# Transnormer attention and a squared-ReLU MLP: the normalised rows turned by VectorE in 32×32 blocks, the product with k^T·v in column strips, and the first loads split by halves of the partitions

## The chip, the cores and the metric

The kernel runs on one core of a Trainium2 chip. The metric is the device time in microseconds of one execution; less is better. TensorE (PE) multiplies matrices and writes to PSUM, VectorE (DVE) and ScalarE (ACT) work on SBUF and PSUM, GpSimd (POOL) does a few set-up steps here, and transfers are issued from the queues of SyncE (SP), ScalarE and GpSimd.

## The reference

All inputs are float32 but the two weight matrices of the second part and its scalars, which arrive as float64.

```python
# q, k, v: (8 batches, 8 heads, 576 positions, 64); g_norm: (64,)
kv  = einsum('bhsd,bhse->bhde', k, v)
out = einsum('bhsd,bhde->bhse', q, kv)
rms = sqrt(mean(out * out, axis=-1) + 1e-6)
x   = (out / rms * g_norm).transpose(0, 2, 1, 3).reshape(4608, 512)
h   = x @ w_in                    # (512, 2048)
g   = s * max(h, 0)**2 + b
res = g @ w_out                   # (2048, 512) -> (4608, 512)
```

## The kernel before

The 4608 rows of x are cut into 36 chunks of 128 rows, and four chunks make a unit; there are nine units. A unit's x is kept transposed in one tile, `xT` (channels on the partitions, four blocks of 128 channels; 512 rows along the free axis)[...]. `mm1` multiplies it with w_in, `mm2` multiplies the squared ReLU with w_out. From the second unit on, both are done with a seven-product scheme on 2×2 blocks, whose sums VectorE forms (`x_sums`, `sums_w_in`); unit 0's first product is done plainly (`mm1_plain`), in 16 slots of 16 PE instructions, because it has to start before the weights are all there.

For a chunk c, `attention(c)` gives three steps.

- `turn` transposes the chunk's q on TensorE (four 128×128 transposes) and copies the result to `qT`.
- `product` multiplies `qT` with `bd_kv`, a block-diagonal tile which holds k^T·v of two heads in each of its four 128×128 blocks. A chunk within one batch takes four matmuls; a chunk that lies in two batches (every ninth) takes eight, with 64 columns of `qT` each (L345). Then it normalises: the square on ScalarE (L354), the sum over a head on VectorE (L356), the root on ScalarE (L359), the reciprocal and the multiplication on VectorE (L361, L362), into `xn`.
- `turn_x` transposes `xn` on TensorE (four transposes, L370) and copies the result into `xT` on ScalarE, with the factor `g_col` (L373).

`kv_product(b)` forms k^T·v of a batch from 72 small matmuls on 64×64 quarters of the array (L297), and copies it to `bd_kv`.

Every engine works through its instructions in the order in which the program writes them (the schedule is manual). During the units, the steps of the next unit's four chunks stand between the slots of `mm2` (the table `side` in `side_of`). At the start there is nothing to lie beside, so the order is written out by hand:

```python
kv_product(0); turn[0](); product[0](); turn[1](); product[1]()
turn[2](); turn_x[0](); turn[3](); product[2](); plus(0)
turn_x[1](); product[3](); slots0[0](); turn_x[2]()
run([(lo, 1), (shift, 1), (plus, 1)]); slots0[1](); turn_x[3]()
```

The weights arrive as float64 words in "raw tiles" of 1 MB, three of which fit at a time. Four steps make a float32 tile of one: `hi` (L160) and `lo` (L165) on ScalarE, `shift` (L169) and `plus` (L179) on VectorE; `plus` frees the buffer and sends the next load. Tiles 0 to 7 are w_in, 8 to 15 are w_out. `tile_at` says after which slot of unit 0 a tile is converted, `more_at` after which its sums are formed. `slots0[0]` needs tile 0 and chunks 0 and 1; `slots0[1]` needs tile 1; `slots0[2]` needs chunks 2 and 3.

The first transfers: `load_kv(0, i)` loads half of batch 0's k and v as four transfers of 288 KB, each to 64 partitions (r = 0 the lower half, r = 1 the upper); k is issued on SP's queue and v on ScalarE's. `load_q(c)` loads two chunks in four transfers, again to 64 partitions each. On GpSimd's queue `g_col` (two transfers), `s_col` and `b_col` are loaded; VectorE multiplies `b_sq` with `b_col` (L278) before it does anything for the attention.

Of the kernel before, what the change touches and what calls it, by code (L numbers as in the profile page):

```python
# [15 lines left out]
def kernel(  # L16
# [34 lines left out]
    nc = tc.nc  # L51
# [235 lines left out]

    def kv_product(b):

        ps = [ps_t.tile([P, 2, D], FP32, name="kv_ps", tag="t") for _ in range(2)]  # L290
        for i in range(2):
            kv = kv_in.pop((b, i))
            for j in range(R):
                for l in range(2):
                    for r in range(2):
                        rows = slice(r * HB, r * HB + HB)
                        nc.tensor.matmul(  # L297
                            ps[r][l * HB : l * HB + HB, i, :],
                            lhsT=kv[rows, 0, l, j, :],
                            rhs=kv[rows, 1, l, j, :],  # L300
                            start=(j == 0),
                            stop=(j == R - 1),
                        )
        for r in range(2):
            for l in range(2):
                ls = slice(l * HB, l * HB + HB)
                if b == 0 and l == 1:
                    nc.vector.tensor_copy(out=bd_kv[0][ls, 2 * r : 2 * r + 2, ls], in_=ps[r][ls])
                else:
                    nc.scalar.copy(bd_kv[b % 2][ls, 2 * r : 2 * r + 2, ls], ps[r][ls])  # L310

    xT = {}

    def attention(c, first=False, between=lambda: None):

        (b, _), (b1, _) = halves(c)
        st = {}

        def turn():
            if first:
                ps = ps_a.tile([P, NP, P], FP32, name="qT_ps", tag="x")
            else:
                ps = ps_t.tile([P, NP, P], FP32, name="qT_ps", tag="t")
            for p in range(NP):
                nc.tensor.transpose(ps[:, p, :], q_in[c][:, 2 * p : 2 * p + 2, :], ident)  # L327
            st["qT"] = attp.tile([P, NP, P], FP32, name="qT", tag="qT")
            if first:
                nc.vector.tensor_copy(out=st["qT"], in_=ps)  # L330
            else:
                nc.scalar.copy(st["qT"], ps)

        def product():
            if first:
                ps = bank_of("att", "xy"[c % 2]).rearrange("p b (m n) -> p (b m) n", m=2)
            else:
                ps = ps_a.tile([P, NP, P], FP32, name="x_ps", tag="x")
            for p in range(NP):
                if b == b1:  # L340
                    matmul(ps[:, p, :], st["qT"][:, p, :], bd_kv[b % 2][:, p, :], True, True)
                    continue
                for s in range(2):
                    half = slice(s * HB, s * HB + HB)
                    nc.tensor.matmul(  # L345
                        ps[half, p, :],
                        lhsT=st["qT"][:, p, half],
                        rhs=bd_kv[(b + s) % 2][:, p, :],
                        start=True,
                        stop=True,  # L350
                    )
            x = ps.rearrange("p c (l d) -> p (c l) d", l=2)
            st["xn"] = attp.tile([P, H, D], FP32, name="xn", tag="xn")
            nc.scalar.activation(st["xn"], x, AF.Square)  # L354
            ss = attp.tile([P, H], FP32, name="ss", tag="ss")
            nc.vector.reduce_sum(ss, st["xn"], axis=mybir.AxisListType.X)  # L356
            between()
            rms = attp.tile([P, H], FP32, name="rms", tag="rms")
            nc.scalar.activation(rms, ss, AF.Sqrt, bias=eps_col, scale=1.0 / D)  # L359
            inv = attp.tile([P, H], FP32, name="inv", tag="inv")  # L360
            nc.vector.reciprocal(inv, rms)  # L361
            nc.vector.tensor_tensor(  # L362
                out=st["xn"], in0=x, in1=inv.unsqueeze(2).to_broadcast((P, H, D)), op=ALU.mult
            )

        def turn_x():
            u, j = divmod(c, 4)
            ps = ps_t.tile([P, NP, P], FP32, name="xT_ps", tag="t")
            for p in range(NP):
                nc.tensor.transpose(ps[:, p, :], st["xn"][:, 2 * p : 2 * p + 2, :], ident)  # L370
# [4 lines left out]
        return [turn, product, turn_x]  # L375

    xs = {}

# [321 lines left out]
    def hi(n):  # L700
        fold_hi(blocks[n])
# [29 lines left out]
    between = [[], [], [(hi, 0), (lo, 0), (shift, 0)], [(hi, 1)]]  # L731

    def run(steps):
        for fn, n in steps:
            fn(n)

    turn, product, turn_x = zip(
        *(attention(c, True, lambda c=c: run(between[c])) for c in range(4))
    )
    kv_product(0)  # L740
    turn[0]()
    kv0p.release()
    gp = ctx.enter_context(tc.tile_pool(name="gp", bufs=NS))
    product[0]()
    turn[1]()
    product[1]()
    turn[2]()
    turn_x[0]()
    turn[3]()
    product[2]()  # L750
    plus(0)
    turn_x[1]()
    product[3]()
    slots0 = [slot for s in range(NS) for slot in mm1_plain(s)]
    slots0[0]()
    turn_x[2]()
    run([(lo, 1), (shift, 1), (plus, 1)])
    slots0[1]()
    turn_x[3]()
    run([(hi, 2), (lo, 2), (shift, 2), (plus, 2)])  # L760

    def side_of(u):

        if u + 1 >= U:
            return {}
        turn, product, turn_x = zip(*(attention(c) for c in range(4 * u + 4, 4 * u + 8)))
        side = {
            2: [turn[0]],
            3: [product[0]],
# [129 lines left out]
```

## Time and profile before

| | |
|---|---|
| median of 20 runs | 1012.0 us (1009.21 to 1015.22) |
| the profiled execution | 1011.98 us, of which 1010.2 us are the span of the core's work |
| PE busy | 978.3 us, 97% of the span |
| VectorE, ScalarE busy | 452.4 us (45%), 203.8 us (20%) |
| granted PE clock, mean | 0.995 |

The page gives busy times of one profiled execution, the chain of work that ended last, and groups of equal instructions. A timeline lists instructions in order, merged where one kind follows another; its columns are the start, the time to the end of the last one, the engine, the line, the tiles and the count. A float32 matmul stands in the records as two instructions, a transpose as one. The records of PE overlap, since matmuls are pipelined; what PE spends on a group is read from its start to the start of the next group.

### The profile page before, as it was taken

The page shows a single profiled execution, that of the slowest core. Times are in us where ns is not written, and L with a number is a line of the kernel's source. Part 1 is how long each engine was busy: PE and PEld are TensorE (multiplying, and loading weights), DVE is VectorE, ACT ScalarE, POOL GpSimd, SP SyncE. Part 2 cuts the span into 40 slices and gives each one's busy share as a digit, 9 for nine tenths or more (in the row PEclk, how much of TensorE's full clock was granted, in tenths as well). Part 3 has the DMA queues.
Part 4 walks back from the last instruction along what each step waited for, and adds up shares of the span by engine and source line. Part 5 has one row for each costly group of instructions (what it writes and reads, how often), then busy time and mean ns, then how long its engine had stood idle before and what let it go on. Part 6 is the DMA issues. An engine that isn't in the chain of part 4 may idle for free.

```text
span 1010.2 us, 13559 instructions
## 1 busy us (share of the span) xinstructions
PE 978.3 (97%) x5826; PEld 860.5 (85%) x5826; DVE 452.4 (45%) x741; ACT 203.8 (20%) x350; POOL 3.9 (0%) x12
## 2 busy tenths in 40 slices
PE   4699989999999999999999999999999999999998
PEld 3588878888888888888888888888888888888887
DVE  1469856553344433443445334533443344433441
ACT  1377122212121111212121212121212111112100
POOL 1000000000000000000000000000000000000000
PEclk9899999999999999999999999999999999999999
DMA  9267945824253324522552265133303250323033
GB/s 254 88 213 248 269 158 120 232 62 144 67 152 94 125 70 139 136 87 91 156 136 84 84 167 136 42 125 119 91 1 134 74 168 1 126 73 136 1 125 84
DMA packets 74028, 121.47 MB, mean 120 GB/s; under 512 B 41584, under 2 KB 47728, under 8 KB 66672
## 3 DMA queue, kind: packets, MB, share of 16 engines
q1 hardware_dynamic: 70096, 118.64, 39.1%
q10 hardware_dynamic: 3744, 1.97, 0.9%
q8 instruction: 46, 0.75, 0.3%
q14 instruction: 14, 0.11, 0.0%
q0 software_dynamic: 128, 0.00, 0.0%
HBM read 103.81 MB, written 16.78 MB: 119 GB/s over the span
## 4 chain that ended last, share of the span: by engine, by line
PE 94%; DVE 3%; DMA 1%; ACT 1%; issue 0%; ACTq 0%; DVEq 0%
PE x_ps L84 51%; PE y_ps L84 30%; PE z_ps L84 8%; PE kv_ps L297 2%; PE qT_ps L327 2%; PE xT_ps L370 1%; DMA kv_sb<-in_v_dram 1%; DMA q_sb<-in_q_dram 1%; DVE ws L186 1%; PE x_ps L345 0%; DVE xs L186 0%; DVE a L183 0%; DVE ws L183 0%; DVE a L418 0%; DVE xn L362 0%
## 5 line engine op out<-in xcount | busy, mean ns | idle before, releaser
L84 PE MATMUL x_ps<-w_sb,a 128*128 128x256 f32 x768 | 172.3, 379 | 0.0
L84 PEld LDWEIGHTS x_ps<-w_sb,a 128*128 128x128 f32 x768 | 144.3, 190 | 18.9 <-issue 0.2
L84 PE MATMUL y_ps<-w_sb,a 128*128 128x256 f32 x640 | 143.4, 379 | 0.0
L84 PEld LDWEIGHTS y_ps<-w_sb,a 128*128 128x128 f32 x640 | 119.4, 190 | 15.2 <-issue 0.2
L84 PE MATMUL x_ps<-xs,ws 128*128 128x256 f32 x512 | 121.1, 379 | 1.3 <-DVE ws L186 1.1
L84 PE MATMUL y_ps<-xs,wb 128*128 128x256 f32 x512 | 120.9, 379 | 0.0
L461 ACT COPY r<-x_ps 128x512 f32<-128x512 f32 x96 | 56.3, 586 | 315.4 <-PE x_ps L84 307.4
L84 PEld LDWEIGHTS x_ps<-xs,ws 128*128 128x128 f32 x512 | 97.1, 190 | 15.2 <-issue 1.4
L84 PEld LDWEIGHTS y_ps<-xs,wb 128*128 128x128 f32 x512 | 97.3, 190 | 13.2
L183 DVE TENSOR_TENSOR a<-y_ps,r 128x512 f32<-128x512 f32 x64 | 44.0, 688 | 122.1 <-ACT r L461 122.1
L84 PE MATMUL x_ps<-xT,wa 128*128 128x256 f32 x384 | 91.0, 384 | 4.0 <-DVE wa L179 3.2
L84 PEld LDWEIGHTS x_ps<-xT,wa 128*128 128x128 f32 x384 | 73.8, 193 | 14.6 <-ACT w_raw L160 3.3
L418 DVE SCALAR_TENSOR_TENSOR a<-a 128x512 f32<-128x512 f32 x96 | 66.5, 692 | 3.3
L533 DVE SCALAR_TENSOR_TENSOR or<-x_ps,s_col,b_row 128x256 f32<-128x256 f32 x52 | 25.0, 482 | 93.0 <-PE x_ps L84 89.7
L84 PE MATMUL x_ps<-xT,ws 128*128 128x256 f32 x256 | 61.1, 381 | 0.0
L84 PE MATMUL z_ps<-xT,wa 128*128 128x256 f32 x256 | 60.5, 379 | 0.0
L356 DVE TENSOR_REDUCE ss<-xn 128x8 f32<-128x512 f32 x36 | 24.6, 684 | 75.7 <-ACT xn L354 75.7
L84 PE MATMUL x_ps<-w_sb,s 128*128 128x256 f32 x256 | 57.8, 380 | 0.0
L494 DVE TENSOR_TENSOR a<-a 128x512 f32<-128x512 f32 x32 | 22.2, 693 | 75.9 <-ACT a L493 75.9
L84 PEld LDWEIGHTS z_ps<-xT,wa 128*128 128x128 f32 x256 | 48.6, 190 | 6.6
L84 PEld LDWEIGHTS x_ps<-xT,ws 128*128 128x128 f32 x256 | 48.1, 190 | 6.7
L84 PEld LDWEIGHTS x_ps<-w_sb,s 128*128 128x128 f32 x256 | 47.6, 190 | 6.1 <-issue 0.2
(96 smaller groups left out, 851.5 us busy)
## 6 DMA issues: line engine op xcount, KB each, us to landing
w_sb<-w SPq DMA_DIRECT2D x56, 1024.0 KB, 4.9
kv_sb<-in_k_dram SPq DMA_DIRECT2D x32, 288.0 KB, 6.0
out_dram<-o SPq DMA_DIRECT2D x72, 128.0 KB, 2.4
q_sb<-in_q_dram SPq DMA_DIRECT2D x66, 128.0 KB, 6.0
w_raw<-in_moe_w_in_dram SPq DMA_DIRECT2D x8, 1024.0 KB, 7.7
w_raw<-in_moe_w_out_dram SPq DMA_DIRECT2D x8, 1024.0 KB, 5.0
kv_sb<-in_v_dram SPq DMA_DIRECT2D x28, 288.0 KB, 7.0
w<-w_up SPq DMA_DIRECT2D x3, 1024.0 KB, 9.9
```

Of the source, the lines that this page charges most:

```text
L84: nc.tensor.matmul(o, lhsT=lhsT, rhs=rhs, start=start, stop=stop, skip_group_check=True)
L183: nc.vector.tensor_tensor(out=o, in0=a, in1=b, op=ALU.add)
L186: nc.vector.tensor_tensor(out=o, in0=a, in1=b, op=ALU.subtract)
L297: nc.tensor.matmul(ps[r][l * HB : l * HB + HB, i, :], lhsT=kv[rows, 0, l, j, :], rhs=kv[rows, 1, l, j, :], start=(j == 0), stop=(j == R - 1),)
L327: nc.tensor.transpose(ps[:, p, :], q_in[c][:, 2 * p : 2 * p + 2, :], ident)
L356: nc.vector.reduce_sum(ss, st["xn"], axis=mybir.AxisListType.X)
L370: nc.tensor.transpose(ps[:, p, :], st["xn"][:, 2 * p : 2 * p + 2, :], ident)
L418: nc.vector.scalar_tensor_tensor(t, t, 0.0, t, ALU.max, ALU.mult)
L461: nc.scalar.copy(st[name], src)
L494: nc.vector.tensor_mul(t, t, t)
L533: nc.vector.scalar_tensor_tensor(o, ps, s_col, other, ALU.mult, ALU.add)
```

## The change

- `load_kv` puts the transfers of the lower half of the partitions on the first queue and those of the upper half on the second, both k and v. `load_q` does the same for q; for chunks 2 and 3 both halves go on SP's queue, behind the first raw tile.
- The raw tiles of w_in are read with channel 4p + c on partition p, block c, in place of 128c + p. The 64 columns of k^T·v are written in another order (e = 4e' + c goes to place 16c + e'), by reading v's columns with a step of four elements.
- `product` is 16 matmuls with 32 columns of `qT` each, the four p of one w going to four 32-partition strips of PSUM. A chunk in two batches takes the same 16.
- The normalising multiplication writes `xn` in runs of 16 elements; `turn_x` is one VectorE transpose of 32×32 blocks from `xn` into `xT`. At every second chunk ScalarE multiplies the two chunks' part of `xT` in place by `g_col`, in four instructions of 128×256.
- `g_col` is now 128×4 and is loaded by eight transfers on GpSimd's queue.
- `product` is split into `product` and `norm`. The order at the start is another, and so are `tile_at` and `more_at`.

```diff
-        for m, src, queue in zip(range(2), (k, v), queues):
-            for r in range(2):
+        for m, src in enumerate((k, v)):
+            for r, queue in enumerate(queues):
                 h = NP * r + 2 * i
                 queue.dma_start(
...
-                queues[i].dma_start(
+                queues[s].dma_start(
                     out=t[s * HB : s * HB + HB, i],
...
-                in_=src.rearrange("(c p) n -> p c n", p=P)[:, :, f * n : f * n + 2 * n],
+                in_=src.rearrange("(p c) n -> p c n", c=KC)[:, :, f * n : f * n + 2 * n],
...
-    g_col = const.tile([P, 1], FP32, name="g_col")
-    for l in range(2):
+    g_col = const.tile([P, KC], FP32, name="g_col")
+    for h in range(H):
+        e = D // KC
         nc.gpsimd.dma_start(
-            out=g_col[l * HB : l * HB + HB, :], in_=g_norm.rearrange("(p o) -> p o", o=1)
+            out=g_col[h * e : h * e + e, :], in_=g_norm.rearrange("(e c) -> e c", c=KC)
         )
...
-                            ps[r][l * HB : l * HB + HB, i, :],
+                            ps[r][l * HB : l * HB + HB, i, :].rearrange("p (c e) -> p c e", c=KC),
                             lhsT=kv[rows, 0, l, j, :],
-                            rhs=kv[rows, 1, l, j, :],
+                            rhs=kv[rows, 1, l, j, :].rearrange("p (e c) -> p c e", c=KC),
...
-            if first:
+            if first and c == 0:
                 ps = ps_a.tile([P, NP, P], FP32, name="qT_ps", tag="x")
...
-            for p in range(NP):
-                if b == b1:
-                    matmul(ps[:, p, :], st["qT"][:, p, :], bd_kv[b % 2][:, p, :], True, True)
-                    continue
-                for s in range(2):
-                    half = slice(s * HB, s * HB + HB)
+            for w in range(4):
+                for p in range(NP):
                     nc.tensor.matmul(
-                        ps[half, p, :],
-                        lhsT=st["qT"][:, p, half],
-                        rhs=bd_kv[(b + s) % 2][:, p, :],
+                        ps[32 * p : 32 * p + 32, w, :],
+                        lhsT=st["qT"][:, p, 32 * w : 32 * w + 32],
+                        rhs=bd_kv[(b if w < 2 else b1) % 2][:, p, :],
...
             nc.vector.tensor_tensor(
-                out=st["xn"], in0=x, in1=inv.unsqueeze(2).to_broadcast((P, H, D)), op=ALU.mult
+                out=st["xn"].rearrange("p h d -> p (h d)").rearrange(
+                    "p (c h e) -> p h c e", c=KC, h=H
+                ),
+                in0=st["x"].rearrange("p h (c e) -> p h c e", c=KC),
+                in1=inv.unsqueeze(2).unsqueeze(3).to_broadcast(shape),
+                op=ALU.mult,
             )
         def turn_x():
             u, j = divmod(c, 4)
-            ps = ps_t.tile([P, NP, P], FP32, name="xT_ps", tag="t")
-            for p in range(NP):
-                nc.tensor.transpose(ps[:, p, :], st["xn"][:, 2 * p : 2 * p + 2, :], ident)
...
-            nc.scalar.activation(xT[u][:, :, j * P : j * P + P], ps, AF.Copy, scale=g_col)
+            to = xT[u][:, :, j * P : j * P + P]
+            nc.vector.transpose(
+                out=to, in_=st["xn"].rearrange("p h d -> p (h d)").rearrange("p (c x) -> p c x", c=KC)
+            )
+            if j % 2 == 1:
+                to = xT[u][:, :, j * P - P : j * P + P]
+                for i in range(KC):
+                    nc.scalar.activation(
+                        to[:, i], to[:, i], AF.Copy, scale=g_col[:, i : i + 1]
+                    )
...
+    two = (nc.sync, nc.scalar)
     for i in range(2):
-        load_kv(0, i, kv0p, (nc.sync, nc.scalar), tag="kv")
-    load_q(0, (nc.sync, nc.scalar))
+        load_kv(0, i, kv0p, two, tag="kv")
+    load_q(0, two)
     send_w()
-    load_q(2, (nc.scalar, nc.scalar))
+    load_q(2)
...
+    turn[0](); turn[1](); product[0](); product[1](); norm[0](); hi(0)
+    turn[2](); norm[1](); shift(0); turn_x[0](); lo(0); plus(0)
+    product[2](); turn[3](); turn_x[1](); product[3](); hi(1); norm[2]()
+    shift(1); lo(1); plus(1); norm[3]()
     slots0 = [slot for s in range(NS) for slot in mm1_plain(s)]
     slots0[0]()
     turn_x[2]()
-    run([(lo, 1), (shift, 1), (plus, 1)])
+    turn_x[3]()
+    for step in (hi, lo, shift, plus):
+        step(2)
     slots0[1]()
-    turn_x[3]()
-    run([(hi, 2), (lo, 2), (shift, 2), (plus, 2)])
...
-    tile_at = {1: 3, 2: 4, 3: 5, 4: 6, 6: 7, 7: 8, 8: 9, 9: 10, 10: 11, 12: 12, 13: 13, 14: 14, 15: 15}
-    more_at = {8: 8, 9: 9, 11: 10, 12: 11, 14: 12, 15: 13}
+    tile_at = {1: 3, 2: 4, 3: 5, 4: 6, 5: 7, 6: 8, 7: 9, 9: 10, 10: 11, 11: 12, 12: 13, 14: 14, 15: 15}
+    more_at = {8: 8, 9: 9, 12: 10, 13: 11, 14: 12, 15: 13}
```

(In the diff the lines that call the start's steps are put several to a line.)

More of the change, by code (lines that the diff above doesn't have):

```diff
@@ L306, in kv_product, with attention @@
                 ls = slice(l * HB, l * HB + HB)
+                to = bd_kv[b % 2][ls, 2 * r : 2 * r + 2, ls]
                 if b == 0 and l == 1:
-                    nc.vector.tensor_copy(out=bd_kv[0][ls, 2 * r : 2 * r + 2, ls], in_=ps[r][ls])
+                    nc.vector.tensor_copy(out=to, in_=ps[r][ls])
                 else:
-                    nc.scalar.copy(bd_kv[b % 2][ls, 2 * r : 2 * r + 2, ls], ps[r][ls])
+                    nc.scalar.copy(to, ps[r][ls])
     xT = {}
-    def attention(c, first=False, between=lambda: None):
+    def attention(c, first=False):
         (b, _), (b1, _) = halves(c)
@@ L351, in product, with norm @@
                     )
-            x = ps.rearrange("p c (l d) -> p (c l) d", l=2)
+            st["x"] = ps.rearrange("p c (l d) -> p (c l) d", l=2)
             st["xn"] = attp.tile([P, H, D], FP32, name="xn", tag="xn")
[L354 to L357, printed above, removed]
+            nc.scalar.activation(st["xn"], st["x"], AF.Square)
+            st["ss"] = attp.tile([P, H], FP32, name="ss", tag="ss")
+            nc.vector.reduce_sum(st["ss"], st["xn"], axis=mybir.AxisListType.X)
+        def norm():
             rms = attp.tile([P, H], FP32, name="rms", tag="rms")
-            nc.scalar.activation(rms, ss, AF.Sqrt, bias=eps_col, scale=1.0 / D)
+            nc.scalar.activation(rms, st["ss"], AF.Sqrt, bias=eps_col, scale=1.0 / D)
             inv = attp.tile([P, H], FP32, name="inv", tag="inv")
             nc.vector.reciprocal(inv, rms)
+            shape = (P, H, KC, D // KC)
             nc.vector.tensor_tensor(
-                out=st["xn"], in0=x, in1=inv.unsqueeze(2).to_broadcast((P, H, D)), op=ALU.mult
+                out=st["xn"].rearrange("p h d -> p (h d)").rearrange(
[4 more added lines that the diff above has]
+                op=ALU.mult,
             )
@@ L367, in turn_x, with whole, run @@
             u, j = divmod(c, 4)
-            ps = ps_t.tile([P, NP, P], FP32, name="xT_ps", tag="t")
-            for p in range(NP):
-                nc.tensor.transpose(ps[:, p, :], st["xn"][:, 2 * p : 2 * p + 2, :], ident)
             if j == 0:
                 xT[u] = xp.tile([P, KC, 2 * TB], FP32, name="xT", tag="xT")
-            nc.scalar.activation(xT[u][:, :, j * P : j * P + P], ps, AF.Copy, scale=g_col)
-        return [turn, product, turn_x]
+            to = xT[u][:, :, j * P : j * P + P]
[8 more added lines that the diff above has]
+                    )
+        return turn, product, norm, turn_x
+    def whole(product, norm):
+        def run():
+            product()
+            norm()
+        return run
     xs = {}
@@ L721 @@
     kv0p = tc.alloc_tile_pool(name="kv0p", bufs=2)
+    two = (nc.sync, nc.scalar)
     for i in range(2):
-        load_kv(0, i, kv0p, (nc.sync, nc.scalar), tag="kv")
-    load_q(0, (nc.sync, nc.scalar))
+        load_kv(0, i, kv0p, two, tag="kv")
+    load_q(0, two)
     send_w()
-    load_q(2, (nc.scalar, nc.scalar))
+    load_q(2)
     for _ in range(2):
         send_w()
[L731 to L739, printed above, removed]
     kv_product(0)
-    turn[0]()
     kv0p.release()
     gp = ctx.enter_context(tc.tile_pool(name="gp", bufs=NS))
+    turn, product, norm, turn_x = zip(*(attention(c, True) for c in range(4)))
+    turn[0]()
+    turn[1]()
     product[0]()
-    turn[1]()
     product[1]()
+    norm[0]()
+    hi(0)
     turn[2]()
+    norm[1]()
+    shift(0)
     turn_x[0]()
+    lo(0)
+    plus(0)
+    product[2]()
     turn[3]()
-    product[2]()
-    plus(0)
     turn_x[1]()
     product[3]()
+    hi(1)
+    norm[2]()
+    shift(1)
+    lo(1)
+    plus(1)
+    norm[3]()
     slots0 = [slot for s in range(NS) for slot in mm1_plain(s)]
@@ L765, in side_of @@
             return {}
-        turn, product, turn_x = zip(*(attention(c) for c in range(4 * u + 4, 4 * u + 8)))
+        turn, product, norm, turn_x = zip(*(attention(c) for c in range(4 * u + 4, 4 * u + 8)))
+        product = [whole(*steps) for steps in zip(product, norm)]
         side = {
```

## The prediction

> **What bounds the kernel now.** I read the busy table first, then the slices, then the chain of waits in order of time, then the timeline of a later unit.
>
> ```profile
> PE 978.3 (97%) x5826; PEld 860.5 (85%) x5826; DVE 452.4 (45%) x741; ACT 203.8 (20%) x350; POOL 3.9 (0%) x12
> PE   4699989999999999999999999999999999999998
> ```
>
> PE is at work in every slice but the first two (50 us), and VectorE is less than half busy overall. So after the start time is won only by taking work off PE; before that, by shortening the chain. The chain of waits, start to first full stretch of PE (columns: start, duration, what):
>
> ```profile
> 2.18 9.49 DMA kv_sb<-in_v_dram
> 11.69 5.29 DMA q_sb<-in_q_dram
> 16.99 0.27 ACT bd_kv L310
> 17.28 0.50 DVE bd_kv L308 x2
> ...
> 37.51 5.14 PE x_ps L84 x16
> 42.66 0.02 issue
> 42.68 0.60 ACT a L440
> ...
> 46.19 5.42 PE y_ps L84 x16
> 51.61 0.02 issue
> ...
> 52.86 3.72 PE x_ps L84 x16
> ```
>
> k^T·v is in SBUF at t0 = 17.78 (17.28 + 0.50), slot 0 starts at 37.51, slot 1 at 46.19, slot 2 at 52.86, and from there PE hardly stops. Between t0 and slot 2 lie 35.1 us, of which slots 0 and 1 would take 2 × 3.46 at the later pace: the rest is four chunks done in series with two weight tiles. The later units, for the price of the attention's steps on PE (timeline, PE alone):
>
> ```profile
> 346.32 0.60 PE L370 MATMUL xT_ps<-ident,xn 128*128 128x128 f32 x4
> 346.85 1.09 PE L345 MATMUL x_ps<-bd_kv,qT 128*64 128x128 f32 x16
> 347.87 3.72 PE L84 MATMUL y_ps<-w_sb,a 128*128 128x256 f32 x16
> 355.32 0.60 PE L370 MATMUL xT_ps<-ident,xn 128*128 128x128 f32 x4
> 355.76 1.06 PE L84 MATMUL x_ps<-bd_kv,qT 128*128 128x128 f32 x8
> 356.65 3.62 PE L84 MATMUL x_ps<-w_sb,s 128*128 128x256 f32 x16
> ```
>
> From start to start: `turn_x` 0.44 (355.76 − 355.32), a plain `product` 0.89 in 8 instructions (111 ns each). In a chunk of two batches the 16 instructions on half strips end 1.11 after the transposes (347.87 − 346.76): 64 ns each, plus about 0.1 idle at the change of form. Two strips thus run at once; one after the other they would take 16 × 111 = 1.78.
>
> [...]SP's kv loads (64 partitions) move 226 to 229 GB/s from 170 to 178 us, the following w2 loads (128) 422 at 180 to 182. [...]for 512 elements I take the 0.69 of L330's 512-element copy.
>
> **The change part by part.**
>
> 1. *PE per chunk, units 1 to 8.* `turn_x` goes: −0.44. `product` becomes 32 instructions in four strips: if four run at once, 32 × 111/4 = 0.89, plus the two changes of form, 0.22 as in L345: 1.11. The 28 plain chunks win 0.22 each (6.2), the four of two batches, already at 1.11, win 0.44 (1.8): **−7.9**. Instructions may not come faster than one per 16 ns (144 of `kv_product` in 2.29 us at 189.30); 28 ns is slower than that, so issue doesn't bind. [...]
>
> 2. *VectorE and ScalarE per chunk.* VectorE gets +0.69, 36 × 0.69 = 25 us on 452. ScalarE gives up 0.69 per chunk and takes four 128×256 multiplications per two chunks (L566, 128×256: 0.47 each, nearer 0.4 at their pitch): 1.6 against 1.4. Both lie under PE's 3.46 per slot. `xT` is read only by `x_sums`, a slot later, and by the next unit, two slots later. Queued behind ScalarE's multiplications, which wait for the transpose, are the next chunk's square and the copy of `qT`. In units 1 to 7 products are two slots apart (8 us), so the added 2.3 us is covered. At the end of unit 0 they are one slot apart (5.0 with their own PE work): slot 10's chain is transpose 1.4, multiplications 1.7, square, sum, root, reciprocal, multiplication 2.6, total 5.7. PE waits once, **+0.7**. Writing `xn` in runs of 16 I cost at nothing (0.69 as before; twice that would still be covered here).
>
> 3. *`kv_product` with a step of four.* 0 if the reads keep up. Twice as slow per read: 144 × (27 − 16) ns = 1.5 each, +12 over eight; four times: +43. I take 0: an instruction takes 0.84 ns per column (256 in 216 ns), four quarters run at once already, and nothing in the trace says that its reads are at their limit.
>
> 4. *Arrival of kv and b.* Before, both queues start with the lower half (k on SP, v on ScalarE), [...]the last of 2.36 MB lands at 14.5; PE ends at 16.7. [...]That isn't the last wait, though. GpSimd's issues take 0.59 each: eight for `g_col` from 2.19 to 6.9. `s_col` now waits for the first of them (same semaphore), `b_col` for the second. Before, the first landed at 9.1, the second at 10.9, `b_col` 8.6 after its issue:
>
> ```profile
> DVE b_sq L278 <- DMA b_col<-in_moe_b_dram: 11.6, 1, 11.6
> ```
>
> VectorE's multiplication by `b_col` stands ahead of its half of the `bd_kv` copies. Before, it started at 12.6 and cost nothing, hidden by kv. Now `b_col` is issued at about 10.5 and lands at about 18.5; copies end at t0' = 18.5 + 0.35 + 0.5 = 19.4. **+1.6** at t0. If the latency shrinks with the load (5 us), 14; if it grows, 21. q and the raw tile 0 (needed at t0' + 5.6) are there by then.
>
> 5. *The order at the start, from t0'.* Durations from the same stretch: PE product 2.0 [...], VectorE copies, sums and multiplications 0.69 (pitch 0.61), square 0.60, root 0.30, hi and lo 1.15, shift 0.69, plus 1.23. VectorE: qT 0 and 1 at 1.3; PE: products at 2.85 and 4.7; sums done 4.2 and 6.05; ScalarE: root 0 5.6, hi 6.75, root 1 7.05, lo 8.15. VectorE: norm 0 7.0, qT 2 7.5, norm 1 8.5, shift 9.1, transpose 9.8, plus 11.0; product 2 9.3; sum 11.7, qT 3 12.3, transpose 12.95. ScalarE multiplies 13.0 to 14.6. Product 3 ends 14.0: slot 0 from 14.05 (before 19.7) to 19.15. Then hi 16.3, norm 2 17.6, plus of tile 1 19.4: slot 1 from 19.45 to 22.9. Norm 3 20.3, slot 0's square 20.9, two transposes 22.2, multiplications to 23.8: slot 2 from **23.3**, against 35.1: **−11.8**. After it, tile 2 is ready at 27.4 (needed 30.3), tile 3 at 30.3 (needed 33.7), so PE goes on. With transposes of 1.2 instead of 0.69, slot 2 comes 2 later.
>
> 6. *`tile_at`, `more_at`, w_in's row order, `load_q` on SP.* The 1 MB tiles keep runs of 2 KB; one tile per slot (3.46) asks 303 GB/s of a rate of 325 to 330 (60 to 70 us). VectorE is 95% busy from 80 to 110 us now and stays so; the last tile is ready 5 us into `mm2`, w_dn is needed 14 us into it. Nothing; if a tile is late, 1 to 3.
>
> Sum: −11.8 + 1.6 + 0.7 − 7.9 = **−17.4**. The profiled execution took 1011.98 (span 1010.2 and 1.8 around it), the median is 1012.0, so the sum can be taken off the median: **994.6**.
>
> **The rivals.**
>
> *A. Strips overlap only in pairs.* Four strips then take what L345 shows for two, 64 ns an instruction: 32 × 64 + 0.1 = 2.15. Per plain chunk +1.26 − 0.44 = +0.82 (28), per mixed chunk +0.6 (4): +25.4, and the start's −9.5 make **1028, slower**. It decides from about 51 ns per instruction[...]. For it: no run shows four strips. Against: `kv_product` on quarters runs at 16 ns where one alone would need 53, so four tiles at once do work.
>
> *B. The strided read of v costs double:* **1006.6**. [...]Against: only the 0.84 ns per column, a slow stream.
>
> *C. b_col lands early and the two halves load side by side:* t0' = 14, **989**. [...]Against: small transfers took 7 to 8.6 while all queues were full.
>
> *D. The start gives only 5* (transposes at twice the price, a tile late): **1000**.
>
> **How the numbers follow.** The forecast 0.52; C 0.15; D 0.15; B 0.10; A, or B at four times (+26), 0.08. Range **984 to 1004**: [...]D with half of B's cost or with steps of 0.1 more per chunk at the high; B and A are left out. Within 0.2% (2 us, about what a measurement of this kernel can tell from no change) I put 0.03, taken from between A and B; faster 0.89, slower 0.08.
>
> **What would show it.** Right: L345 on 32-column strips at about 1.1 from start to start; no xT_ps on PE; `b_sq` starting at 16 to 19 us, and after kv's last matmul; slot 2's start near 42.7; kv_product at 2.3 in later units. Wrong: strips at 2 us, kv_product at 4, PE waiting for `xT` at a unit's first slot, or a `b_sq` that starts before 14.

## The result, and the profile after

The changed kernel takes 1001.73 us (median of 7 runs, 1001.30 to 1002.88) against 1012.99 for the kernel before on the same chips: ratio 0.9895, 95% interval 0.9879 to 0.9911. It is faster by 11.3 us, not by the 17.4 forecast. The profiled execution has a span of 1000.1 us against 1010.2, so the trace has 10.1 us to account for. Runs of the kernel before spread over about 11 us (1005.8 to 1016.9 over all that are on record, with a mean granted clock, where it is listed, of 0.988 to 0.997), those of the changed kernel over 1.6 (0.994 to 0.998); what is read below from one profiled execution of each, the start above all, can be a few us more or less in another run. The busy table and the PE row of the slices, after:

```profile
PE 977.5 (98%) x6514; PEld 848.3 (85%) x6514; DVE 474.5 (47%) x777; ACT 208.8 (21%) x386; POOL 6.7 (1%) x18
PE   4899999999999999999999999999999999999998
```

PE's busy time is what it was (978.3 before), although 36 × 4 transposes of x are gone from it. So something on PE has become dearer by about as much as they cost. VectorE has 22 us more, and in the later units no wait of PE goes with it. The second slice is an 8 where it was a 6: the start is fuller.

**The start.** Timeline of the start, one line per merged group (start, us to the end of the last, engine, line, tiles, count, and in brackets the idle time before it with its releaser):

```profile
13.17 2.43 PE L299 MATMUL kv_ps<-kv_sb 64*64 64x64 f32 x72 [1.69 <-DMA kv_sb<-in_v_dram]
14.88 0.29 DVE L279 TENSOR_SCALAR b_sq<-b_sq,b_col 128x128 f32<-128x128 f32 x1 [13.84 <-DMA b_col<-in_moe_b_dram]
...
15.98 0.50 DVE L311 COPY bd_kv<-kv_ps 64x128 f32<-64x128 f32 x2 [0.81 <-ACT bd_kv L313]
...
28.23 5.41 PE L84 MATMUL x_ps<-xT,wa 128*128 128x256 f32 x16
...
34.13 3.69 PE L84 MATMUL y_ps<-xT,wb 128*128 128x256 f32 x16 [0.49 <-DVE inv L362]
37.66 3.62 PE L84 MATMUL x_ps<-xT,wa 128*128 128x256 f32 x16
```

k^T·v is in SBUF at t0 = 15.98 + 0.50 = 16.48 (17.78 before). `b_sq` is multiplied at 14.88, ahead of the end of PE's last matmuls for k^T·v at 15.60: `b_col` holds nothing up. Slots 0, 1 and 2 start at 28.23, 34.13 and 37.66; before they started at 37.51, 46.19 and 52.86. Slot 2 is 15.2 us earlier.

**A later unit.** Timeline, PE alone:

```profile
279.04 4.41 PE L299 MATMUL kv_ps<-kv_sb 64*64 64x64 f32 x144
283.38 1.99 PE L84 MATMUL x_ps<-xT,ws 128*128 128x256 f32 x8
...
332.29 1.08 PE L345 MATMUL x_ps<-bd_kv,qT 128*32 128x128 f32 x32
333.30 3.72 PE L84 MATMUL y_ps<-w_sb,a 128*128 128x256 f32 x16
336.86 0.60 PE L331 MATMUL qT_ps<-ident,q_sb 128*128 128x128 f32 x4
```

The same `kv_product` in the kernel before:

```profile
295.56 2.33 PE L297 MATMUL kv_ps<-kv_sb 64*64 64x64 f32 x144
297.82 1.99 PE L84 MATMUL x_ps<-xT,ws 128*128 128x256 f32 x8
```

`product` on four strips takes 1.01 from start to start (32 ns per instruction against 111 for a plain one), so the four strips do run at once: the trace has the first four instructions start within 20 ns of each other, and the next four 0.11 us later. But two other prices have changed. The 16 instructions after it take 3.56 (336.86 − 333.30), where such a group without strips before it takes 3.45 to 3.46. And `kv_product` takes 4.34 to the next group's start at 283.38, 30.1 ns per instruction, where the same 144 took 2.26 (297.82 − 295.56) to 2.33 before.

**Where the 10.1 us come from**, in spans and starts of the two profiled executions:

| step | forecast, us | measured, us | how it is worked out |
|---|---|---|---|
| start, to slot 2 | −10.2 | −15.2 | 37.66 − 52.86 |
| `kv_product`, seven in the units | 0 | +14.4 | 30.4 − 15.9, the seven of each kernel from start to next start |
| PE per chunk, units 1 to 8 | −7.9 | −5.1 | 28 × 0.12 + 4 × 0.44, from the experiment with the old product |
| wait at the end of unit 0 | +0.7 | +0.5 | PE's wait for `xn` in product 3 |
| a stop in unit 0 of before that is gone | – | −4.5 | 3.56 − 8.10, below |
| sum | −17.4 | −9.9 | the spans: −10.1 |

The last row but one was not in the forecast. In the kernel before, PE stops once within a group of `mm2` in unit 0. Timeline of before, PE alone:

```profile
128.77 0.92 PE L84 MATMUL x_ps<-w_t,a 128*128 128x256 f32 x3
132.27 4.76 PE L84 MATMUL x_ps<-w_t,a 128*128 128x256 f32 x13 [2.59 <-issue]
136.87 0.60 PE L327 MATMUL qT_ps<-ident,q_sb 128*128 128x128 f32 x4
```

From start to start these 16 instructions take 8.10 (2.6 of stop, and the granted clock at 0.57 from 132 to 136). In the changed kernel the same 16 run without a stop from 115.46 to 119.02, 3.56. "issue" says that PE waited for nothing that the profile shows. The row of the table compares one execution of each kernel; whether every run of the kernel before stops here is not on record.

### The profile page after: what moved, and what is told of

Read it like the earlier page. It is cut to its first block, busy times and chain, and to the rows that moved or that the text cites. A ratio compares the mean times of both kernels' runs of the same rounds, so it can differ in the third digit from the quotient of the medians.

```text
span 1000.1 us, 15059 instructions
## 1 busy us (share of the span) xinstructions
PE 977.5 (98%) x6514; PEld 848.3 (85%) x6514; DVE 474.5 (47%) x777; ACT 208.8 (21%) x386; POOL 6.7 (1%) x18
## 4 chain that ended last, share of the span: by engine, by line
PE 94%; DVE 2%; DMA 2%; SPq 1%; ACT 0%; issue 0%; ACTq 0%; DVEq 0%
PE x_ps L84 48%; PE y_ps L84 30%; PE z_ps L84 8%; PE x_ps L345 3%; PE kv_ps L299 3%; PE qT_ps L331 1%; DMA w_raw<-in_moe_w_in_dram 1%; DMA kv_sb<-in_k_dram 1%; DVE ws L186 1%; SPq L114 0%; SPq L135 0%; DVE xs L186 0%; DVE ws L183 0%; DVE a L183 0%; DVE a L437 0%
## 5 line engine op out<-in xcount | busy, mean ns | idle before, releaser
L84 PEld LDWEIGHTS x_ps<-xT,wa 128*128 128x128 f32 x384 | 74.0, 193 | 10.8 <-ACT xT L384 0.3
```

The source lines that it names most:

```text
L84: nc.tensor.matmul(o, lhsT=lhsT, rhs=rhs, start=start, stop=stop, skip_group_check=True)
```

## The experiments

Each is an edit of the changed kernel unless it says otherwise. Times are medians, or that of a single execution where no range is given; spans are those of the profiled execution.

### v read in its natural order

What failed is most likely `kv_product`; the first question is whether the strided read of v is the cause. Here v is read, and PSUM written, in natural order, and the four copies from PSUM to `bd_kv` permute the columns instead.

```diff
-                            ps[r][l * HB : l * HB + HB, i, :].rearrange("p (c e) -> p c e", c=KC),
+                            ps[r][l * HB : l * HB + HB, i, :],
-                            rhs=kv[rows, 1, l, j, :].rearrange("p (e c) -> p c e", c=KC),
+                            rhs=kv[rows, 1, l, j, :],
...
-                to = bd_kv[b % 2][ls, 2 * r : 2 * r + 2, ls]
+                to = bd_kv[b % 2][ls, 2 * r : 2 * r + 2, ls].rearrange("p i (c e) -> p i c e", c=KC)
+                src = ps[r][ls].rearrange("p i (e c) -> p i c e", c=KC)
```

> The changed kernel, but the matmuls of k^T v read v and write PSUM in the natural order, and the four copies from PSUM into bd_kv put the columns into their new order instead. Theory 'the step of four floats slows the reads': the 144 instructions of a later kv product go back from 4.34 us to about 2.3 us, seven of them give 14.4 us, so 987 us (span 986), unless the copies, which now read PSUM with a step of four, become dearer than 0.26 us each and PE waits for them. Rival 'the form of the tiles or the strips around the product slows it': kv products stay at 4.3 us and the time at 1001.7.

Measured: 987.7 us (987.54 to 988.66), ratio to before 0.9765 (0.9740 to 0.9789); span 985.8, 14.3 less than the changed kernel's. `kv_product` in a later unit (timeline, PE):

```profile
275.09 2.33 PE L299 MATMUL kv_ps<-kv_sb 64*64 64x64 f32 x144
```

It is back at its price of before. The stop of unit 0 is absent here too. The permuting copies cost no more than plain ones: ScalarE's four `bd_kv` copies of a later unit, which follow one another, take 1.07 us (from 277.47), 1.08 in the changed kernel (from 283.49). So the +14.4 is the strided access of these matmuls, and this version, which computes the same thing, beats both kernels.

### Steps of two and of eight

The strided read could be dear because it isn't contiguous at all, because the distance is long, or because the price sets in at some step and then stays. Both kernels leave v's columns, and with them the channels, in another order than x needs; only their times are of use.

```diff
-... .rearrange("p (c e) -> p c e", c=KC),   -... .rearrange("p (e c) -> p c e", c=KC),
+... .rearrange("p (c e) -> p c e", c=2),    +... .rearrange("p (e c) -> p c e", c=2),
```

> The changed kernel with v read with a step of two floats instead of four (the channels of x then stand in an order that does not fit g and w_in). Only the time of the kv products is asked. [...]2.3 to 3.3 us instead of 4.34. Rival 'any read that isn't contiguous, or any three-dimensional pattern, costs the same': 4.3 us.

The second kernel has `c=8` in both places.

> The changed kernel with v read with a step of eight floats instead of four (the channels of x then stand in an order that does not fit g and w_in). [...]4.3 us again. Rival 'the cost grows with the distance': 6 to 8 us per kv product.

Measured: 988.87 us with a step of two (span 987.1), 1002.74 with eight (span 1001.0). `kv_product` with a step of two:

```profile
276.26 2.35 PE L299 MATMUL kv_ps<-kv_sb 64*64 64x64 f32 x144
```

and with a step of eight:

```profile
279.65 4.46 PE L299 MATMUL kv_ps<-kv_sb 64*64 64x64 f32 x144
```

Two is free (2.28 from start to next start, 2.26 in natural order), four and eight cost the same (4.34 and 4.39): about 2.1 us more per `kv_product`. So it isn't the missing contiguity, and from four to eight the price doesn't grow with the distance; a price that sets in above two and then stays fits. One that comes with every multiple of four elements would fit as well; a step of three or five, which would tell, was not run. Why such a read is slow, these runs don't show. The edit changes the write to PSUM along with the read of v, but with a run of 32, 16 or 8 elements every write is contiguous, so the read is what is left.

### The old product with the new transposes

This separates the strips from the rest: `product` is again four matmuls of 128 columns (eight on half strips in a chunk of two batches), and everything else stays; what reaches `xT` isn't x^T then.

```diff
-            for w in range(4):
-                for p in range(NP):
+            for p in range(NP):
+                if b == b1:
+                    matmul(ps[:, p, :], st["qT"][:, p, :], bd_kv[b % 2][:, p, :], True, True)
+                    continue
+                for s in range(2):
...
```

> The changed kernel with the product of before: four matmuls of 128 columns of qT (eight of 64 in a chunk of two batches) in place of 16 on strips; the VectorE transposes stay, so what reaches xT is not x^T. It asks what the strips cost. Theory 'the strips overlap four at a time and cost only the two changes of form': a plain product goes from 1.10 to 0.89 us, 28 in the units and four at the start, so 6 to 7 us less: 995 to 996. Rival 'the strips lose more than their own time, by the waits around them': 990 or less.

Measured: 993.63 us (993.31 to 994.55), ratio to before 0.9828 (0.9798 to 0.9858), 8.1 less than the changed kernel: between the 995 to 996 and the 990 that I had set against each other, and nearer to the first. Timeline of a later unit, PE:

```profile
338.34 1.05 PE L84 MATMUL x_ps<-bd_kv,qT 128*128 128x128 f32 x8
339.23 3.62 PE L84 MATMUL x_ps<-w_sb,s 128*128 128x256 f32 x16
342.68 0.60 PE L331 MATMUL qT_ps<-ident,q_sb 128*128 128x128 f32 x4
```

`product` takes 0.89, and the group after it 3.45, not 3.56. In the changed kernel the group ahead of the strips takes 3.55 from start to start (328.74 to 332.29), 0.10 more than such a group elsewhere. A product on strips therefore costs about 0.10 before it, 1.01, and 0.11 after it: 1.21 to 1.22. Twenty-eight plain chunks at 0.32 are 9.0 us, against 8.7 in the spans (1000.1 and 991.4), of which 0.8 lie in the start and unit 0, so the price per chunk is good to about a tenth of itself. The forecast's 1.11 left the last 0.1 out, although the trace of before had it: the group after the half strips takes 3.56 there (347.87 to 351.43), the one after a plain product 3.46 (356.65 to 360.11). So per plain chunk the change wins 0.44 + 0.89 − 1.21 = 0.12, and in the four mixed chunks, whose half strips already paid on both sides, 0.44.

### Strips one after the other

Do the four strips overlap because neighbouring instructions go to different strips? The two loops are swapped, so that four matmuls, which are eight instructions, in a row go to one strip.

```diff
-            for w in range(4):
-                for p in range(NP):
+            for p in range(NP):
+                for w in range(4):
```

> The changed kernel with the loops over p and w exchanged in the product: eight instructions in a row go to the same strip. Theory 'neighbouring instructions overlap because they lie in different strips': now they follow each other at 111 ns, 32 x 111 = 3.55 us a product instead of 1.01, so 32 x 2.5 = 80 us more: 1075 to 1085. Rival 'PE overlaps them whatever their order, or 32 ns is a limit of issue': 1.0 us and 1002.

Measured: 1047.55 us (span 1045.8). Timeline, PE:

```profile
336.27 2.46 PE L345 MATMUL x_ps<-bd_kv,qT 128*32 128x128 f32 x32
338.66 3.72 PE L84 MATMUL x_ps<-w_sb,a 128*128 128x256 f32 x16
```

From start to start 2.39 us, 75 ns per instruction, against 32 in the kernel's order. The order of the loops is worth 46 us: the direction was right, but 75 isn't the 111 that I expected. The single starts in this product's trace tell why. The records don't name the strip, but the starts fall into four trains of eight. Within a train they lie 109 to 133 ns apart, so instructions of one strip do follow one after the other, as expected. But each train starts 0.47 us after the one before, when that one still has three of its eight instructions to start. So two strips at a time overlap for part of the way: 3 × 0.47 + 0.99 from the last train's start to the next group make 2.39. Why a strip starts that far ahead and no further stays open.

### A wide product that reads with a step of four

In `kv_product` four streams share the array. Is one of them held up by its own reads, or do they get in each other's way? Here the kernel with the old product reads `bd_kv` with a step of four, one stream at a time; like that kernel it puts into `xT` something other than x^T.

```diff
-                    matmul(ps[:, p, :], st["qT"][:, p, :], bd_kv[b % 2][:, p, :], True, True)
+                    matmul(
+                        ps[:, p, :].rearrange("p (c e) -> p c e", c=KC), st["qT"][:, p, :],
+                        bd_kv[b % 2][:, p, :].rearrange("p (e c) -> p c e", c=KC), True, True,
+                    )
```

> The kernel wide_product (four full-width matmuls per product, VectorE's transposes kept, so what reaches xT is not x^T), whose matmuls now read bd_kv with a step of four floats. It asks whose limit the step meets. Theory 'each stream alone is held back': with four quarters at once an instruction of 64 columns took 4 x 30.1 = 120 ns, 1.9 ns per column; 128 columns would take 240 ns instead of 111, a plain product 1.9 us instead of 0.89, 28 of them +29 us: about 1022. Rival 'only the four streams together are held back': 0.47 ns per column for one of them, less than the 0.84 it takes anyway: 0.89 us and 993.6 as before.

Measured: 1019.64 us (span 1017.9). Timeline, PE:

```profile
355.54 1.98 PE L84 MATMUL x_ps<-bd_kv,qT 128*128 128x128 f32 x8
357.33 7.09 PE L84 MATMUL x_ps<-w_sb,a 128*128 128x256 f32 x32
```

1.79 us for 8 instructions, 224 ns each where 111 was usual: a single stream is held to 224/128 = 1.75 ns per column (0.87 before). In `kv_product` each quarter has 4 × 30.1/64 = 1.88 ns per column. So most of the limit lies on each stream by itself, and little is left for four of them together. This is one execution, and its 1019.6 is near the 1022 that this theory gave.

### The old loads

The first loads as before: k on SP's queue, v on ScalarE's, and chunks 2 and 3 of q on ScalarE's queue.

```diff
-        for m, src in enumerate((k, v)):
-            for r, queue in enumerate(queues):
+        for m, src, queue in zip(range(2), (k, v), queues):
+            for r in range(2):
...
-                queues[s].dma_start(
+                queues[i].dma_start(
...
-    load_q(2)
+    load_q(2, (nc.scalar, nc.scalar))
```

> The changed kernel with the first loads as before: k on SP's queue and v on ScalarE's, both starting with the lower half of the partitions; q chunk by chunk, chunks 2 and 3 on ScalarE's queue. Theory 'the halves on two queues bring b_col and kv earlier': kv's matmuls end at 16.7 us again instead of 15.6, b_col lands 7 to 8.6 us after its issue at about 10.5 instead of 4.2 us, so b_sq starts near 18 and delays the bd_kv copies; slot 2 starts 2 to 4 us later than 37.66; 1004 to 1006 us. Rival 'the queues make no difference, the order of the steps does it all': b_sq and slot 2 as in the changed kernel, within 0.5 us; 1001.7.

Measured: 1005.71 us (1005.26 to 1006.00), 4.0 more than the changed kernel; ratio to before 0.9939 (0.9922 to 0.9956). Timeline of its start:

```profile
24.69 0.63 PE L331 MATMUL qT_ps<-ident,q_sb 128*128 128x128 f32 x4 [3.69 <-DMA q_sb<-in_q_dram]
...
41.05 3.62 PE L84 MATMUL x_ps<-xT,wa 128*128 128x256 f32 x16
```

Slot 2 is 3.4 later. Of that 1.5 is t0 (17.96 against 16.48). The rest, 1.9, lies between t0 and slot 2, where PE now waits for chunk 2's q: the four transfers of chunks 2 and 3 land 5.6 to 12.4 us after their issue on ScalarE's queue, the last of chunk 2's 9.9; in the changed kernel they land after 6.5 to 8.1. `b_col` lands 5.6 us after its issue against 4.2. So the new loads do help, by about a fifth of the start's gain. The run takes both parts of the edit back at once: t0 can come from the halves of k and v, the wait for q is that of the queue on which chunks 2 and 3 are loaded, and how the 3.4 us divide between the two was not measured. From 2 to 8 us the new loads move no more bytes than those of the kernel before (168, 232 and 217 GB/s against 203, 229 and 210), and from 8 to 14 us 282, 317 and 268 against 217, 224 and 209 in the kernel before.

### The new loads alone

The same edit the other way round, in the kernel before.

> The kernel before with only the new load queues (lower halves on SP, upper on ScalarE, q of chunks 2 and 3 on SP). Theory 'the halves bring kv earlier by themselves': the last kv load lands at 13.2 instead of 14.5, the bd_kv copies end about 1.3 us earlier than 17.78 and slot 2 starts about 1.3 us before 52.86: 1010.7 against 1012. Rival 'the loads only pay with the new order, in which chunk 2 and tile 0 are asked for earlier': within 0.5 us of before.

Measured: 1012.62 us (1005.38 to 1014.93), ratio 1.0001 (0.9984 to 1.0018): nothing. Timeline of its start, PE:

```profile
35.95 6.57 PE L84 MATMUL x_ps<-xT,wa 128*128 128x256 f32 x16 [3.41 <-DVE wa L179]
...
46.07 6.65 PE L84 MATMUL y_ps<-xT,wb 128*128 128x256 f32 x16 [3.11 <-DVE wb L179]
```

Slot 0 does start 1.6 us earlier than in the kernel before. But slots 0 and 1 then take 6.57 and 6.65 us where they took 5.13 and 5.41 before, and slot 2 comes 1.1 later, at 53.98. The granted clock, from 38 to 42 and from 46 to 50 us, is 0.53 and 0.50 here; in the kernel before it is 0.70 and 0.66. In this execution the gain of the loads is given back there, in slots whose clock is lower. That the loads bring the lower clock is not shown: the two executions have mean clocks of 0.991 and 0.995, and runs of the kernel before alone range from 0.988 to 0.997. What the runs show is that the medians are equal.

### The old order

The changed kernel with the order, `tile_at` and `more_at` of before.

```diff
-    turn[1]()
     product[0]()
-    product[1]()
...
+    turn[1]()
+    product[1]()
...
+    slots0[1]()
...
```

> The changed kernel with the order of before at the start (each product with its normalising in turn, tile 0 between chunk 2's sum and root, tile 1 after slot 0) and the old tile_at and more_at; loads, strips and VectorE transposes stay as changed. Theory 'the order at the start is most of the gain there': slot 2 starts at 48 to 50 instead of 37.66, so 1012 to 1014. Rival 'VectorE's transposes and the shorter products shorten the start by themselves': slot 2 at 40 to 42, 1004 to 1006.

Measured: 1019.32 us (1015.37 to 1021.48), ratio to before 1.0078 (1.0056 to 1.0099): slower than before; span 1017.7, 17.6 more than the changed kernel. Timeline of its start, PE:

```profile
34.57 6.20 PE L84 MATMUL x_ps<-xT,wa 128*128 128x256 f32 x16 [4.83 <-ACT xT L384]
...
44.83 6.17 PE L84 MATMUL y_ps<-xT,wb 128*128 128x256 f32 x16 [4.06 <-DVE wb L179]
...
58.65 3.62 PE L84 MATMUL y_ps<-xT,wb 128*128 128x256 f32 x16
```

Slots 0 and 1 each start after a wait of 4 to 5 us and take over 6 us in place of 3.45, with a granted clock of 0.50 from 34 to 38 us and 0.52 from 46 to 50. Slot 3 starts at 58.65, in the changed kernel at 41.11: 17.5 of the 17.6 arise in the start, and hardly anything in the later steps of `tile_at` and `more_at`. The order is worth more than I expected of it (10 to 12), and the slow slots point to the clock as the rest.

### The old order, with PE kept at work

To separate the two: the same kernel with 20 matmuls in PE's waits, whose results nobody reads.

```diff
+    def keep_warm(n):
+        ps = ps_t.tile([P, DM], FP32, name="d_ps", tag="t")
+        for _ in range(n):
+            matmul(ps[:, :TB], ident, bd_kv[0].rearrange("p n m -> p (n m)")[:, :TB], True, True)
...
+    keep_warm(6)
...
```

> The kernel old_order with 20 matmuls of 256 columns that nobody reads (6 before slot 0, 8 after it, 6 after slot 1), in PE's waits. Theory 'PE's clock is lowered after its waits, and slots 0 to 2 pay for it': they take 3.5 to 4 us each instead of 6.2, 6.2 and 5.2, and slot 3 starts 5 to 8 us before 58.65: 1012 to 1014 instead of 1019.3. Rival 'the slots are slow for another reason': the added matmuls only fill the waits, or delay the slots by 1 to 3 us: 1019 to 1022.

Measured: 1013.32 us (1012.53 to 1015.18), 6.0 less than without them; ratio to before 1.0015 (1.0000 to 1.0029). Timeline of its start, PE:

```profile
33.72 3.72 PE L84 MATMUL x_ps<-xT,wa 128*128 128x256 f32 x16 [0.83 <-ACT xT L384]
...
41.41 3.72 PE L84 MATMUL y_ps<-xT,wb 128*128 128x256 f32 x16 [0.52 <-DVE wb L179]
...
51.27 3.62 PE L84 MATMUL y_ps<-xT,wb 128*128 128x256 f32 x16
```

Twenty matmuls more, and slot 3 starts 7.4 us earlier. The windows view of the kernel without them, from 46 to 50 us (busy times of the engines, then the granted clock PEclk, the share of DMA and the rate):

```profile
46.00:50.00 4.00, 4.00 (x12) 3.17 (x11) 0.00 (x0) 0.00 (x0) 0.00 (x0) 0.52 0.82 262
```

and with them:

```profile
46.00:50.00 4.00, 4.00 (x19) 3.13 (x19) 1.21 (x3) 2.85 (x6) 0.00 (x0) 1.00 0.09 35
```

The clock goes from one half to full; from 34 to 38 us, in slot 0, it is likewise 0.50 and 1.00. Of the order's 17.6 us, 6.8 (the spans 1017.7 and 1010.9) are the clock that PE loses in its waits. The other 10.8 are what is left, in the main the waits themselves, near the −11.8 of the forecast's step 5. In the kernel without the added matmuls the low clock (0.50 from 34 to 38 us, 0.52 from 46 to 50) stands behind waits of 4.83 and 4.06 us. But shorter waits stand before a low clock too: 3.11 us before 0.66 in the kernel before, 3.11 before 0.50 with the new loads alone, 2.59 before 0.57 at the stop in unit 0. So these runs show no length of wait below which it is harmless.

### Tile 1 earlier

In the version with v in natural order, slot 1 still waits 2.2 us on VectorE. Here tile 1 is converted before product 3.

```diff
-    turn_x[1]()
-    product[3]()
...
-    norm[2]()
-    shift(1)
...
+    turn_x[1]()
+    shift(1)
...
+    norm[2]()
+    product[3]()
```

> The kernel plain_v_read with tile 1 converted before product 3 in place of after it: hi and lo of tile 1 fill ScalarE's wait for the second transpose, shift and plus follow that transpose on VectorE, norm 2 comes after them. In plain_v_read slot 0 ends at 32.1 and slot 1 starts at 34.28, on plus of tile 1. Theory 'tile 1 is what slot 1 waits for, and ScalarE has the time': slot 1 from about 32.1, slot 2 from about 35.5 instead of 37.8, 985.4 us. Rival 'tile 1's load lands too late (24.5) or ScalarE's multiplications for slot 0 are pushed back': slot 0 starts later and the time stays within 0.5 of 987.7.

Measured: 987.65 us (987.03 to 988.20), ratio to before 0.9750 (0.9718 to 0.9781): the same as without the edit. Timeline, PE, without it:

```profile
28.38 3.72 PE L84 MATMUL x_ps<-xT,wa 128*128 128x256 f32 x16
34.28 3.69 PE L84 MATMUL y_ps<-xT,wb 128*128 128x256 f32 x16 [2.19 <-DVE inv L363]
```

and with it:

```profile
28.71 5.41 PE L84 MATMUL x_ps<-xT,wa 128*128 128x256 f32 x16 [0.55 <-ACT xT L385]
33.95 3.62 PE L84 MATMUL y_ps<-xT,wb 128*128 128x256 f32 x16
```

The 985.4 that I expected did not come. The wait at slot 1 is gone, but slot 0 takes 5.24 us in place of 3.7, so slot 1 starts only 0.3 earlier, and the span is 0.3 shorter (985.5 against 985.8), less than the runs of either kernel differ among themselves. That the edit makes slot 0 slow is not shown: in the changed kernel, which has not got this edit, slot 0 is just as slow (28.23 to 33.64, then a wait of 0.49), so its pace differs between executions without the edit too.

## Why the prediction was right and where it was wrong

The direction and the main source were right: the start carries the gain. The total missed by 7.1 us. By far the largest error is one step that was put at nothing, +14.4. That the total still came within the stated range is in part luck: the start gave 5.0 more than forecast, and −4.5 came from a stop that stood in no step. Of the signs of being wrong that the prediction named, one came true, `kv_product` at 4.

- **Step 3, `kv_product`: the step that failed.** It was put at 0 because 0.84 ns per column is a slow stream and nothing in the trace showed it at a limit. But a trace with no strided read cannot show such a limit. The case stood in the text as rival B (the strided read at double the price), with its chance at 0.10. Its price was small as well: B took 1.5 us each for eight, and the runs show about 2.1 for seven in the units, **+14.4**. Natural order takes it away (2.26 us per `kv_product`), a step of two is free (2.28), and one of eight costs what four costs (4.39 and 4.34); the reason for the slow read was not shown.
- **Step 1, PE per chunk: right in kind, mis-sized.** `turn_x` is gone, the strips overlap four at a time (an estimate of the author's in the forecast, 32 ns per instruction in the trace) and rival A is refuted. The term that was too small is the change of form, from full-width matmuls to strips and back: 0.10 before the product, 0.12 within it (1.01 against the 0.89 of four strips at once), 0.11 in the group after it, 0.33 in all where 0.22 was put. The forecast read the product from its start to the next start and left the last out. −5.1 instead of −7.9.
- **Step 2, VectorE and ScalarE.** The transpose takes 703 ns (forecast 690, an estimate from a copy of 512 elements), 25.2 us in all; writing `xn` in runs of 16 costs nothing (692 ns as before); the one wait, in unit 0, is 0.54 (forecast 0.7). No PE wait for `xT` shows in the later units. All about as worked out.
- **Step 4, kv and `b_col`: wrong by 2.9 us.** t0' was put at 19.4 and is 16.48. The latency of `b_col` was taken from before, 8.6 us, and is 4.2 here. In these runs it goes with the time of the issue: issued at 3.9 us it took 8.6 with the old loads and 7.8 with the new loads alone, issued at 10.6 with the new loads 4.2, at 11.4 with the old 5.6. The forecast's own case of a latency that shrinks was the nearer one. So rival C (that the two halves load side by side was an estimate of the author's) was right that `b_col` isn't the last wait; its t0' of 14 was too early, because PE's last matmuls end at 15.6. From 8 to 12 us, with one half of the partitions per queue, the loads move 282 and 317 GB/s against the 217 and 224 of before, 36% more. The kernel before also loaded from two queues, both of which start with the lower half; how much of the 36% the halves alone make was not measured.
- **Step 5, the order: right, a little short.** From t0 to slot 2, 21.2 (forecast 23.3, before 35.1): −13.9 in place of −11.8. Products 0 and 1 take about 1.2 and 1.1 where the 2.0 of before was used (2.04 and 2.07 there, with a granted clock of 1.00 from 18 to 22 and 24 to 26 us). With step 4 that makes −15.2 in place of −10.2. Rival D is out.
- **Step 6, tiles.** The PE row of the slices has a 9 in every slice from the third to the last but one; the slots from 37.66 to 86.00 follow each other at 3.45; no late tile, as forecast.
- **Not in any step:** the stop of 2.6 us in unit 0 of before and the slow instructions behind it, −4.5. It was in the trace of before, and the forecast did not price its going. Its cause stays open. One lead: a 16 KB packet of the instruction queue (q8) starts at 129.9, within the stop, and at 131.2 within that of the new loads alone; but such packets also start where PE goes on (116.7 in the changed kernel), so this shows no cause. It also shows with the new loads alone (2.8 us), and in none of the kernels built on the changed one, the one with the old order, the one with the old loads and those with the cheap `kv_product` among them; so, as far as one execution of each can say, it hangs on none of these three by itself.

## What to carry to other kernels

When an edit makes TensorE read a float32 operand with a step, read in a trace what the step costs: here one of two was free (2.28 us per `kv_product`), and four and eight took nearly twice as long (4.34 and 4.39); let a copy from PSUM, which has to be made anyway, do the permuting (1.07 us for four copies, 1.08 without it). When a kernel mixes full-width matmuls with matmuls on strips, read the groups before and after the strips too: here they paid 0.10 and 0.11 us of the change. At a start that is a chain of waits, count the slow instructions after each wait along with the wait: here they were 6.8 of the order's 17.6 us.

## What the runs showed that I had not expected

- A step of four float32 holds a single stream to 1.75 ns per column (0.87 without it), and four streams at once to 1.88 each; from a step of four to one of eight the price hardly grows (4.34 to 4.39 us per `kv_product`).
- Filling PE's waits with 20 unread matmuls made a kernel 6.0 us faster.
- The 32 instructions of a product on 32-column strips take 32 ns each if neighbouring matmuls lie on different strips, and 75 ns if eight instructions in a row share one; then at most two strips ran at once.
- A load of 0.5 KB on GpSimd's queue landed 7.8 to 8.6 us after its issue when that was at 3.9 us, and 3.9 to 5.6 when it was at 10.4 to 11.4.
